# S4 convolution and GEGLU block on one Trainium2 core: a tenth table of y exponentials in the place of an early weight read, with the order of the first 1482 places redone

## The chip, the cores and the metric

The kernel runs on one core of a Trainium2 chip. The metric is the device time of one execution in microseconds (us). Within a core, TensorE (PE) multiplies matrices, VectorE (DVE), ScalarE (ACT) and GpSimd (POOL) work on tiles, and DMAs are issued from the queues of SyncE (SP), ACT and POOL. Each engine works through its own instructions in the order in which the program lists them and waits on semaphores for the others.

## The reference

A block with adaptive layer norm: an S4 convolution, then a gated feed-forward layer. L = 2048 tokens, D = 448 channels, N = 256 states per channel, 1792 hidden features. All inputs are float32.

```python
mod = (silu(c) @ w_mod)              # six rows of 448: sa, ca, ga, sb, cb, gb
h = layernorm(x) * (1 + ca) + sa
P = exp(dt * A * l)                  # A = A_re + i A_im, for every channel, state and step l
K = einsum("dn,dnl,dn->dl", C, P, dt * B).real
y = irfft(rfft(h, 2 L) * rfft(K, 2 L))[:L] + h * Dskip
x = x + ga * y
h = layernorm(x) * (1 + cb) + sb
g, u = h @ w_gate, h @ w_up
x = x + gb * ((gelu(g) * u) @ w_down)
```

## The kernel before

**Stages.** In the first 40 us the parameters of the first quarter of the channels are prepared. Then, up to about 341 us, the convolution's kernel K is *generated* in 56 steps of eight channels each, while the transforms of the input and of finished parts of K run beside it. A *tail* to about 381 us ends the transforms, applies the inverse, adds the residual and norms the first 512 tokens. From there to the end come the gate, up and down projections, 512 tokens at a time, in float16 pairs of a high and a low part.

**Generation.** The powers exp(dt A l) are split into magnitudes and angles, and each of these into a coarse and a fine part of l. PE multiplies the prepared operand `lt` (read from the scratch tensor `lh_d`) by the constants `ea` and `rd` into `pg`; ACT turns `pg` into the table `my` (y exponentials, L663, 128 x 1024 float32, 4 KB in a partition) for each step, into the smaller `mx` (x exponentials, L645) for pairs of steps, and into sines and cosines `fg` (L689, L693, L700). DVE multiplies `mx` and `fg` to `tx` (L722) and `my` and `fg` to `ty` (L726), and PE multiplies these to `kg` (L749). Then `kg` is copied to `ke` (L483 on DVE, L481 on ACT), turned by L772 and copied to `ako`, the transforms' operand. Exponentials and sines need different function tables on ACT, so a switch between them is an `ACT_TABLE_LOAD`. The `my` tiles form a ring of `NMY` places in the pool `tabl`: up to that many y exponentials can be done ahead of their products, which allows several of them behind one switch.

**The operand.** `prep` works out the operand of a quarter of the channels on DVE and ACT. Two puts (L596) write it to `lh_d`, a read of ones (L515, task `pad`) fills the rows behind it, and the reads at L621 (`lt0` for magnitudes, `lt1` for angles) fetch it turned. `lt0` waits for the first put and for the ones.

**First weights.** The gate and up weights come in tiles `w` of 128 x 4 x 256 float32 (4 KB in a partition). The function `weight` issues the read (L1332; `w.le` on SP for three early ones, `w.la` on ACT's queue for the next three, then `w.ld` on SP), ACT makes the float16 high part `wr` (L1345), and DVE the low part (L1349, L1350). The very first of them, for `cb` and `k` zero, has its own place in the pool `ahead`, which is there from the start, and no dependence; it is read near 55 us. The others share a ring of three places in `ws`, a pool that is opened when the generation's pools are closed (`ev.end`).

**Tail and first tiles.** The norm's result `xn` (L1451, L1452) of each of four blocks of 128 tokens is cast to its high part `hl` (L483 or L481, task `co.h0`), DVE takes the low part (L1460, L1461), PE turns both (L1470) and ACT or DVE copies them to `ht`. The gate and up tiles of the first half (two of the four blocks) start as soon as these two are turned: each is ten and one matmuls for gate and up (L1530, L1524) into a `pq` tile, of which there are two. ACT's gelu of the gate (L1537, `ge`) and DVE's product with the up part (L1544, `fq`) give the `pq` tile free. Small filler matmuls (L1036, tasks `spin`) run on PE in the tail.

**What sets the order.** Nothing is scheduled at run time. The table `PLACE` gives every task a number, and a letter for its engine where it could run on several (a ACT, d DVE, p POOL, s SP); tasks are written out by ascending number. The list of a name counts its tasks in the order in which the program adds them.

## Time and profile before

| what | value |
|---|---|
| timed runs | 776.79, 777.25, 779.4 us; median 777.25 us |
| profiled execution | 776.06 us, with a span of 774.3 us |
| granted PE clock, mean | 0.995 |
| busy in the span | PE 724.2 us (94%), DVE 591.3 (76%), ACT 459.7 (59%), POOL 8.5 (1%) |
| DMA | 139.87 MB, mean 181 GB/s |

The span runs from the first to the last instruction of the profile; the execution's own time has 1.76 us around it. The share of busy time is a mean over stages that differ: PE is at work for 94% of the span, though in the generation another engine sets the pace. In the prediction, rows of groups give the line, engine, operation, tiles and shape, the count, then busy time and mean nanoseconds of one, then the idle time ahead of the group and what ended it; rows of a timeline give the start, the duration, the engine and line, and in brackets the wait ahead.

### The profile page before, as it was taken

To read this page: it belongs to the slowest core of one execution; us is meant where nothing else is said; L and a number is where in the kernel's file an instruction comes from. 1 tells how busy PE (TensorE), PEld (TensorE's weight loads), DVE (VectorE), ACT (ScalarE), POOL (GpSimd) and SP (SyncE) were. 2 spreads that over 40 slices of the span, in tenths; PEclk is the share of its full clock that TensorE was granted. 3 is DMA by queue.
4 is the path that set the end of the run, shared out by engine and by line. 5 is a ranking of instruction groups with operands and counts; after the bars stand their busy time and mean duration, and the time that the engine had idled before them with its cause. 6 is when DMAs were issued, how large, how long until landed. Compare 5 with 4: busy or idle time off the path is not lost.

```text
span 774.3 us, 19010 instructions
## 1 busy us (share of the span) xinstructions
PE 724.2 (94%) x8166; PEld 442.5 (57%) x8166; DVE 591.3 (76%) x891; ACT 459.7 (59%) x613; POOL 8.5 (1%) x23
## 2 busy tenths in 40 slices
PE   2877889998899999989999999999999999999997
PEld 1333554443677777677874445444694446944487
DVE  6999999999999999979958932578774577144743
ACT  5899999999999999952646620244312433022330
POOL 0000000000000000003000000000000000000000
PEclk9999999999999999999999999999999999999999
DMA  9764777997888687897787791455247224013201
GB/s 265 193 187 160 214 184 222 276 272 236 247 230 252 180 233 239 275 310 208 235 269 257 221 235 79 146 166 211 98 82 211 96 96 136 14 50 99 77 2 60
DMA packets 103950, 139.87 MB, mean 181 GB/s; under 512 B 34388, under 2 KB 85492, under 8 KB 103866
## 3 DMA queue, kind: packets, MB, share of 16 engines
q1 hardware_dynamic: 100436, 132.53, 58.2%
q10 hardware_dynamic: 2950, 5.38, 2.0%
q8 instruction: 64, 1.05, 0.6%
q0 software_dynamic: 480, 0.75, 0.3%
q14 instruction: 20, 0.16, 0.1%
HBM read 100.39 MB, written 36.01 MB: 176 GB/s over the span
## 4 chain that ended last, share of the span: by engine, by line
PE 73%; ACT 12%; DVE 8%; DMA 4%; issue 2%; SPq 1%; DVEq 0%; ACTq 0%
PE pq L1530 32%; PE pq L1630 9%; PE pd L1599 4%; PE pg L676 4%; PE pf L1104 4%; PE kg L749 3%; ACT my L663 3%; DVE ty L726 2%; PE pq L1524 2%; PE pf L985 2%; PE pf L1093 2%; PE kg L772 2%; PE pf L1206 2%; ACT fg L689 2%; DMA us<-uo 2%
## 5 line engine op out<-in xcount | busy, mean ns | idle before, releaser
L1530 PE MATMUL pq<-ht,wr 128*128 128x512 f16 (+1 forms) x1200 | 248.3, 365 | 0.1
L1530 PEld LDWEIGHTS <-wr 128*128 128x128 f16 x1200 | 114.6, 98 | 128.5 <-issue 11.3
L726 DVE TENSOR_TENSOR ty<-my,fg 128x2048 f32<-128x2048 f32 x56 | 127.3, 2284 | 0.4 <-ACT fg L693 0.3
L1537 ACT ACTIVATE ge<-pq 128x512 f32<-128x512 f32 (+1 forms) x60 | 34.0, 566 | 106.9 <-PE pq L1524 71.3
L1544 DVE TENSOR_TENSOR fq<-ge,pq 128x512 f32<-128x512 f32 (+1 forms) x60 | 39.0, 650 | 72.6 <-PE pq L1530 45.0
L1556 ACT ACTIVATE hh<-fq 128x1024 f16<-128x1024 f32 (+1 forms) x49 | 46.7, 962 | 65.6 <-DVE fq L1544 47.0
L1630 PE MATMUL pq<-d,hh 128*128 128x224 f16 x476 | 68.9, 259 | 0.0
L722 DVE TENSOR_TENSOR tx<-mx,fg 128x1024 f32<-128x1024 f32 x56 | 67.6, 1218 | 0.2 <-ACT fg L700 0.2
L749 PE MATMUL kg<-ty,tx 128*32 128x64 f32 x3584 | 61.6, 222 | 4.4 <-DVE tx L722 1.7
L749 PEld LDWEIGHTS kg<-ty,tx 128*32 128x32 f32 x3584 | 53.2, 111 | 21.3 <-issue 5.9
L1559 DVE TENSOR_TENSOR hlo<-fq,hh 128x1024 f16<-128x1024 f32 (+1 forms) x49 | 53.7, 1106 | 12.9 <-ACT hh L1556 12.7
L1630 PE MATMUL pq<-d,hlo 128*128 128x224 f16 x238 | 61.6, 259 | 0.0
L689 ACT ACTIVATE fg<-pg 128x1024 f32<-128x1024 f32 x56 | 57.6, 1040 | 0.5 <-PE pg L676 0.3
L663 ACT ACTIVATE my<-pg 128x1024 f32<-128x1024 f32 x56 | 56.2, 1032 | 0.4
L1630 PEld LDWEIGHTS <-hh 128*128 128x128 f16 x560 | 54.1, 98 | 0.9 <-issue 0.2
L693 ACT ACTIVATE fg<-fg,small 128x1024 f32<-128x1024 f32 x36 | 42.2, 1180 | 0.0
L1104 PE MATMUL pf<-q,fc 128*128 128x160 f32 x264 | 41.5, 307 | 0.0
L1104 PEld LDWEIGHTS pf<-q,fc 128*128 128x128 f32 x264 | 36.5, 190 | 5.3 <-issue 2.2
L676 PEld LDWEIGHTS <-lt 64*128 64x128 bf16 x304 | 17.7, 95 | 35.0 <-issue 22.7
L676 PE MATMUL pg<-ea,lt 64*128 64x512 bf16 x152 | 31.3, 390 | 6.5 <-ACT fg L689 3.0
L1747 ACT ACTIVATE d<-fq 128x896 f16<-128x896 f32 x14 | 13.2, 946 | 39.7 <-PE pd L1599 27.3
L985 PE MATMUL pf<-ui,fu 128*128 128x448 f32 x66 | 31.2, 576 | 1.2 <-DVE uo L993 0.5
(210 smaller groups left out, 1119.2 us busy)
## 6 DMA issues: line engine op xcount, KB each, us to landing
wr<-w_d SPq DMA_DIRECT2D x21, 896.0 KB, 4.6
fc<-in_k_fc SPq DMA_DIRECT2D x20, 576.0 KB, 4.2
u_d<-so SPq DMA_DIRECT2D x32, 224.0 KB, 3.0
ui<-u_d SPq DMA_DIRECT2D x10, 672.0 KB, 6.0
fq<-in_wd SPq DMA_DIRECT2D x14, 448.0 KB, 4.1
w<-in_wgu SPq DMA_DIRECT2D x11, 512.0 KB, 4.6
us<-uo SPq DMA_DIRECT2D x22, 240.0 KB, 4.5
q<-us SPq DMA_DIRECT2D x22, 240.0 KB, 4.5
```

What stands on the lines that cost most here:

```text
L663: A.activation(yb.tile.rearrange("p h (n k) -> p n h k", n=2), pb.tile.rearrange("p (n h k) -> p n h k", n=2, h=2), AF.Exp)
L676: T.matmul(pa[:, nh * 512:nh * 512 + 512], w, x, start=(k == 0), stop=(k == 2))
L689: A.activation(fb.tile[:, 0].rearrange("p x (n k) -> p n x k", n=2), pb.tile.rearrange("p (n x k) -> p n x k", n=2, x=2), AF.Sin, scale=TW ...
L722: V.tensor_mul(tx.tile, xb.tile[:, xm, None, :].to_broadcast([128, 2, 512]), fb.tile[:, :, 0])
L726: V.tensor_mul(ty.tile, yb.tile[:, :, None, :].to_broadcast([128, 2, 2, 512]), fb.tile[:, None, :, 1].to_broadcast([128, 2, 2, 512]))
L749: T.matmul(kg[32 * g:32 * g + 32, 2 * (s % 2) + q, :64], tx[:, r, nh, 4 * q + g], ty[:, 0:4:3, nh, 4 * q + g] if r else ty[:, 1:3, nh, 4 * ...
L985: T.matmul(pb.tile, fu.tile[:, i], ui.tile[:, EORD[e0 + i] % 32 - s0], start=True, stop=True)
L1104: T.matmul(pz.tile[:, e % 32 - sl0], fc.tile[:, i, 1 + t], pp.tile[:, t, i], start=(t == 0 and e != 32), stop=(t == 1 and e != 0))
L1530: T.matmul(pb.tile[k][:, ts], wr.tile[:, 4 * lo + t, k, c0:c0 + 128], ht[:, m, ts], start=f % 2 == 0 and i == 0, stop=f % 2 == 1 and i == 9)
L1556: A.activation(hg.tile[0][:, cb, c], fq.tile[:, c], AF.Copy)
L1559: V.tensor_sub(hg.tile[1][:, cb, c], fq.tile[:, c], hg.tile[0][:, cb, c])
L1630: T.matmul(bank(k)[:, m], x[:, p, q[0], ts], w[:, p, q[1]], start=new and m == 0 and p == 0 and z == 0, skip_group_check=True, stop=i in ( ...
```

## The change

The ring `my` gets ten places in `tabl` instead of nine. In `weight`, the case of the very first tile is gone: it takes a place of the ring `ws` like its neighbours, and its read waits for the end of the generation (`EV["end"]`) and for `t_x`, a task of the tail. `PLACE` has new numbers for the tasks up to about place 1481, and some tasks change between ACT and DVE; from 1482 on the order is as before. The code below `weight` moves up by one line, so L1332 becomes L1331, and so on.

```diff
-    NMY, NMX = 9, 5
+    NMY, NMX = 10, 5
...
         early = cb + k < 2 and cb < 2
-        zero = cb + k == 0
 
         def ld():
-            wb.tile = (ahead if zero else POOLS["ws"]).tile([128, 4, 256], FT, name="w")
+            wb.tile = POOLS["ws"].tile([128, 4, 256], FT, name="w")
             (dma if early or cb >= PRE else adma)(wb.tile, a["wgu"][cb, :, k])
...
-            t1 = add("w.le", {"SP": 0.42}, -1350 + k + 2 * cb, ld, [] if zero else [EV["end"], t_x], [wb], kb=540)
+            t1 = add("w.le", {"SP": 0.42}, -1350 + k + 2 * cb, ld, [EV["end"], t_x], [wb], kb=540)
...
-    "w.le": "196 1300 1323",
+    "w.le": "1284 1311 1310",
...
-    "co.h0": "1393d 1404a 1432d 1435a",
+    "co.h0": "1395a 1404a 1437a 1436d",
```

Three places of the order bear on the prediction. The first is SP's queue at the start of the program: the read of ones (L515) and the first put (L596, 112x1536), with the reads of the constants `au`, `rd`, `ea` and of the operand `lt`. Before:

```order
L806 DMA fg<-in_w_mod 112x1792 x3
L515 DMA lh_d<-in_k_one 224x512
L596 DMA lh_d<-lh 112x1536
L487 DMA au<-in_k_au 128x128
L487 DMA rd<-in_k_rd 128x1025
L487 DMA ea<-in_k_ea 128x1536
L621 DMA lt<-lh_d 64x7x128 x2
```

After:

```order
L806 DMA fg<-in_w_mod 112x1792 x3
L596 DMA lh_d<-lh 112x1536
L515 DMA lh_d<-in_k_one 224x512
L487 DMA rd<-in_k_rd 128x1025
L487 DMA ea<-in_k_ea 128x1536
L487 DMA au<-in_k_au 128x128
L621 DMA lt<-lh_d 64x7x128 x2
```

The ones now stand behind the put.

The second is ACT where the gate and up tiles begin: the gelus `ge` of the first tiles, the cast `hl` of a block, its turned copies `ht`, the weight read `w` and the conversion `wr`. Before:

```order
L481 ACTIVATE hl<-xn 128x448
L481 ACTIVATE hl<-xn 128x64
L1537 ACT_TABLE_LOAD
L1537 ACTIVATE ge<-pq_5471 128x256
L481 ACTIVATE ht<-pd 128x4x128
L1537 ACTIVATE ge<-pq_5501 128x256
L481 ACTIVATE ht<-pd 128x4x128
L1537 ACTIVATE ge<-pq_5568 128x256
L481 ACTIVATE ht<-pd 128x4x128
L1345 ACTIVATE wr<-w 128x4x256
```

After:

```order
L1536 ACT_TABLE_LOAD
L1536 ACTIVATE ge<-pq_5472 128x256
L1331 DMA w<-in_wgu 128x1024
L1536 ACTIVATE ge<-pq_5517 128x256
L481 ACTIVATE hl<-xn 128x448
L481 ACTIVATE hl<-xn 128x64
L481 ACTIVATE ht<-pd 128x4x128
L1358 DMA w_d<-wr 128x3584
L481 ACTIVATE ht<-pd 128x4x128
L1344 ACTIVATE wr<-w 128x4x256 x2
L1536 ACTIVATE ge<-pq_5578 128x256
```

The cast moved from ahead of the first gelu to behind the second, the weight read from earlier to between them, and two conversions stand ahead of the third gelu where one stood behind it.

The third is DVE in the same stretch, with the casts and low parts of the normed blocks (`hl`), the products `fq` and the low parts `wr` of the weights. Before:

```order
L483 CAST hl<-xn 128x448
L483 CAST hl<-xn 128x64
L1460 TENSOR_TENSOR hl<-xn,hl 128x448
L1461 COPY hl<-hl 128x64
L1544 TENSOR_TENSOR fq<-ge,pq_5472 128x256
L1349 SCALAR_TENSOR_TENSOR wr<-w,wr 128x3x256
L1350 SCALAR_TENSOR_TENSOR wr<-w,wr 64x256
L1544 TENSOR_TENSOR fq<-ge,pq_5502 128x256
```

After, from the second product to the third:

```order
L1543 TENSOR_TENSOR fq<-ge,pq_5518 128x256
L1459 TENSOR_TENSOR hl<-xn,hl 128x448
L1460 COPY hl<-hl 128x64
L1459 TENSOR_TENSOR hl<-xn,hl 128x448
L1460 COPY hl<-hl 128x64
L1348 SCALAR_TENSOR_TENSOR wr<-w,wr 128x3x256
L1349 SCALAR_TENSOR_TENSOR wr<-w,wr 64x256
L483 COPY ht<-pd 128x4x128
L1348 SCALAR_TENSOR_TENSOR wr<-w,wr 128x3x256
L1349 SCALAR_TENSOR_TENSOR wr<-w,wr 64x256
L1543 TENSOR_TENSOR fq<-ge,pq_5579 128x256
```

Both low parts of the blocks, and two low parts of weights, stand between the second and the third product now.

On PE the order at this point is the same in both: the first tile, the second, the turn of eight blocks of `hl` (L1470 before, L1469 after), then the third.

340 rows, old and new, of the table PLACE are left out of this document.

## The prediction, made before the change was run

> **What bounds the kernel now.** I read the table of windows first, cut where the character of the work changes; its columns are the window, its length, the busy time of PE, PEld, DVE, ACT and POOL with instruction counts, the granted PE clock, the DMA share and GB/s.
>
> ```profile
> 0.00:10.00 10.00, 0.00 (x0) 0.00 (x0) 4.38 (x14) 4.38 (x9) 0.88 (x10) 1.00 0.81 268
> 10.00:40.00 30.00, 20.97 (x80) 8.43 (x81) 27.60 (x62) 24.46 (x34) 0.00 (x0) 0.94 0.78 207
> 40.00:341.00 301.00, 275.36 (x5132) 175.64 (x5133) 294.47 (x338) 290.35 (x362) 0.00 (x0) 0.99 0.80 232
> 341.00:381.00 40.00, 38.48 (x488) 32.48 (x480) 33.49 (x70) 15.97 (x34) 7.58 (x13) 1.00 0.73 213
> 381.00:700.00 319.00, 319.00 (x1988) 179.95 (x1986) 195.42 (x350) 107.07 (x153) 0.00 (x0) 1.00 0.50 153
> 700.00:774.30 74.30, 70.37 (x495) 45.97 (x494) 35.99 (x60) 17.42 (x24) 0.00 (x0) 0.99 0.16 51
> ```
>
> Row three is the generation of the S4 kernel. DVE is busy 294.47 of 301 us and ACT 290.35, so DVE sets the pace, with 6.5 us idle, and ACT follows closely. Row four is the tail: the last transforms, the convolution's output and the norm ahead of the gate and up projections; PE has 1.5 us idle. From 381 us PE has no gap for 319 us. The order of the program is unchanged from shortly after that point, so a delay of the first gate and up matmuls goes to the end in full, and nothing the change does later can help.
>
> The next view, the groups, says where the tables stand in this, and the list of DVE's waits says what the 6.5 us are:
>
> ```profile
> L726 DVE TENSOR_TENSOR ty<-my,fg 128x2048 f32<-128x2048 f32 x56 | 127.3, 2284 | 0.4 <-ACT fg L693 0.3
> L663 ACT ACTIVATE my<-pg 128x1024 f32<-128x1024 f32 x56 | 56.2, 1032 | 0.4
> L722 DVE TENSOR_TENSOR tx<-mx,fg 128x1024 f32<-128x1024 f32 x56 | 67.6, 1218 | 0.2 <-ACT fg L700 0.2
> ```
> ```profile
> DVE q L1097 <- PE pf L1093: 1.5, 3, 0.7
> ...
> DVE tx L722 <- ACT fg L700: 0.2, 1, 0.2
> ```
>
> The last figures of the group rows are idle time ahead of the group: ACT stood 0.4 us in all ahead of its 56 y exponentials, and DVE 0.4 us ahead of the 56 products that use the tables. So nobody waits for a tenth table now. The list of waits has 13 rows from the first to the last shown, together 5.2 us, and none of them names `my`.
>
> **The change, part by part.** *The tenth table.* Counting y exponentials issued less y products issued in the two orders, at most nine tables were held before, and ten are held now, but the tenth only once. The switches between exponentials and sines stay: 43 table loads on ACT in both. The table is therefore worth what a shifted ACT order is worth. DVE's work up to the last `tx` product, counted with the mean duration of each form, goes from 353.29 to 353.53 us (these means overlap a little at the ends); ACT's to its last sine differs by 0.07. So the generation costs +0.2 by work. Its waits can fall by at most the 5.2 us listed and can grow by as much; none of the listed waits is removed by a rule of the change, so I take 0 for them, with both ends kept.
>
> *The start.* The copy of ones into the transposed operand (L515) is issued before the first put (L596) now, and behind it after the change. The first read of `lt` (L621) needs both.
>
> ```profile
> 5.88 0.65 SPq L515 DMA_DIRECT2D lh_d<-in_k_one  x1
> 18.25 0.33 SPq L596 DMA_DIRECT2D lh_d<-lh  x1
> ...
> 22.05 1.34 SPq L621 DMA_DIRECT2D lt<-lh_d  x2
> ```
> ```profile
> DMA to landing us min/median/max: 3.7/6.6/6.8
> ```
> ```profile
> DMA to landing us min/median/max: 7.7/7.7/7.7
> ```
> ```profile
> 25.90 1.28 ACT L663 ACT_TABLE_LOAD   x1
> 27.19 1.02 ACT L663 ACTIVATE my<-pg 128x1024 f32<-128x1024 f32 x1
> ```
> ```profile
> 25.23 0.71 PE L658 MATMUL pg<-ea,lt 64*128 64x512 bf16 x2
> 19.27 0.62 DVE L878 BATCH_NORM_STATS2 st<-xt 128x6 f32<-128x448 f32 x1
> ```
>
> The two landing rows are those of L596 (eight issues) and of L515 (four). The put is the step that `lt` waits for: 18.25 + 3.7 is 21.95, and the read starts at 22.05. After the change DVE has one more pair of statistics (0.62 + 0.18 us) ahead of the product that the put sends, so the put starts near 19.05 and the ones near 19.45. If they land in 3.7 us, `lt` is read at 23.2, 1.1 later. The first exponentials have cover for that: their matmul ends at 25.94, but ACT, held by a table load, starts them at 27.19, 1.25 later. That gives 0. If the ones need the 7.7 us of their only reading (a later copy, in the generation, where puts take 6.6 as well), the read starts at 27.2, 5.2 later, and 3.9 are left behind the cover. I take 0, since the put at 3.7 us is the nearest row in time, queue and target, and keep 3.9 as the upper end. [...]
>
> *The first weights.* Their read goes from near 55 us to the tail, behind the end of the generation, and their table of 4 KB no longer has a place of its own. ACT is busy 15.97 of 40 us in the tail and needs them 30 us later, so the read and its conversion lie in idle time: 0, and if the cover were gone, a landing of some 5 us. SP carries one DMA of 512 KB more in the tail ahead of the early read of the convolution's result: about 0.5 us of issue, an estimate from the 0.33 that such an issue takes on ACT's queue below and the 0.65 of L515 above, on a step whose first matmul is at 361.20, with other PE work on both sides. Also 0.
>
> *The tail.* The generation hands over here, and PE picks up:
>
> ```profile
> 339.54 1.22 DVE L722 TENSOR_TENSOR tx<-mx,fg 128x1024 f32<-128x1024 f32 x1
> 344.50 1.60 PE L1188 MATMUL pf<-ako,fc 128*128 128x128 f32 x12 [0.70 <-ACT ako L481]
> 361.20 0.76 PE L1404 MATMUL pd<-yi,ai 128*64 128x320 f32 x4
> ```
>
> From 344.5 to 380.8 PE runs with hardly a gap and the same matmuls in both orders, some of them filler, until the last normed block is turned. On that chain the cast of the first block moves from DVE (0.49) to ACT (0.72), and two small DVE steps of the last block stand behind a neighbour's. I work out +0.35 us for the first gate matmuls, with ends 0 and 1.5 (PE's idle time there, once more).
>
> *The first gate and up tiles.* Here the new order puts a wait where there was none.
>
> ```profile
> 380.80 2.34 PE L1530 MATMUL pq<-ht,wr 128*128 128x256 f16 x20
> 382.91 0.72 ACT L481 ACTIVATE hl<-xn 128x448 f16<-128x448 f32 x2 [1.00 <-DVE xn L1452]
> 383.40 2.36 PE L1530 MATMUL pq<-ht,wr 128*128 128x256 f16 x20
> 384.29 0.49 DVE L483 CAST hl<-xn 128x448 f16<-128x448 f32 x2
> 384.94 0.38 ACT L1537 ACTIVATE ge<-pq 128x256 f32<-128x256 f32 x1
> 385.60 0.61 PE L1470 MATMUL pd<-idenh,hl 128*128 128x128 f16 x8
> 386.04 2.35 PE L1530 MATMUL pq<-ht,wr 128*128 128x256 f16 x20
> ```
>
> Before, the third block's cast (`hl`, ACT at 382.91) was ready 2 us before PE turned it at 385.60, straight behind the second tile. After, ACT's order is first gelu, weight read, second gelu, then that cast. The second gelu needs the second tile complete, and PE's next instructions are the turn. So PE stands while ACT does 0.38 of gelu and 0.72 of cast, with some 0.1 of hand-over: 1.2 us. No other work is queued on PE between, and the gelu can't start sooner, so I count it in full. It is the largest term and the firmest.
>
> *The third weights.* Their read on ACT's queue (L1332, whose landing is the last row here) stands behind the first gelu after the change, and their conversion ahead of the third:
>
> ```profile
> 379.27 0.33 ACTq L1332 DMA_DIRECT2D w<-in_wgu  x1
> 389.46 1.05 ACT L1345 ACTIVATE wr<-w 128x1024 f16<-128x1024 f32 x1
> 390.55 0.96 DVE L1349 SCALAR_TENSOR_TENSOR wr<-w,wr 128x768 f16<-128x768 f32 x1 [0.74 <-ACT wr L1345]
> 391.52 0.42 DVE L1350 SCALAR_TENSOR_TENSOR wr<-w,wr 64x256 f16<-64x256 f32 x1
> 389.05 0.42 DVE L1544 TENSOR_TENSOR fq<-ge,pq 128x256 f32<-128x256 f32 x1 [0.73 <-ACT ge L1537]
> ```
> ```profile
> DMA to landing us min/median/max: 3.9/4.6/5.3
> ```
>
> Shifted by the terms above, the first gelu ends near 384.2, the read lands near 389.0, two conversions (1.05 each) run on ACT to about 391.15 and the low part (0.96 + 0.42) on DVE to about 392.9. The third product (0.42) stands behind it and ends at 393.3; PE needs its buffer for the fifth tile at about 391.55 + 1.55 = 393.1. That is +0.3 with rounding up, 0 if the read lands at 3.9, and +1 at 5.3 with the gelus of that stretch queued behind.
>
> *Sum.* 0.2 + 0 + 0 + 0.35 + 1.2 + 0.3 = **+2.05 us** on the profiled execution's 776.06 (774.3 of span and 1.76 around it), or 778.1. The median of the three timed runs is 777.25, 1.2 higher, and the prediction is of such a median: **779.3**.
>
> **The rivals.** *Faster: the generation's waits go.* DVE's 5.2 us of listed waits, 1.5 of it for the inverse transform's matmuls at L1093, depend on what stands beside what, and the whole order ahead of the tail is new. If it empties all of them and the tail costs the +2 above, the time is 777.25 + 2.05 − 5.2 = 774.1. It is below no change's bound (2.3 us, see below) from 4.4 us of gain on, and any less lands within it. For it: 10.6 us of ACT's time in that window is idle too, so neither engine is at its limit. Against it: nothing in the change removes the matmuls or the ACT steps that end those waits, and DVE's work is 0.2 longer.
>
> *No change: the stall is made up.* If ACT is ready earlier in the tail and 1 to 2 us of waits go in the generation, the sum is 0 to +1: 777.3 to 778.3.
>
> *Slower: the ones land late.* By their own reading of 7.7 us the exponentials start 3.9 later. DVE can fill only part of that with statistics and copies (27.60 of 30 us busy already); by the rest, 2 to 3.9, the time is 781.3 to 783.2. It decides from a landing of about 4.9 us on.
>
> *The clock.* It falls in one place:
>
> ```profile
> 32.00:34.00 2.00, 1.76 (x10) 0.50 (x9) 1.97 (x5) 1.97 (x6) 0.00 (x0) 0.66 0.99 293
> 34.00:36.00 2.00, 1.80 (x8) 0.71 (x8) 1.97 (x7) 1.98 (x3) 0.00 (x0) 0.50 0.42 152
> ```
>
> That follows windows in which PE was idle some 40%. If the new stall brought the same 0.5 for 4 us, it would cost another 2 us: 781.3. Against it, a gap of 1.2 us among full windows is far shorter than that stretch. [...]
>
> *The table doesn't do what it says.* The tenth is held once, and ACT waited only 0.4 us for anything there; then the table is worth nothing by itself and what is left is the order. My forecast contains this.
>
> **How the numbers follow.** Forecast as summed (778.1 to 780.5): 0.40. Faster by the waits: 0.17, of which 0.12 past the bound. No change, made up: 0.15. Ones late: 0.18. New waits in the generation: 0.06. Clock: 0.04. A measurement of this kernel can tell about 0.3% (2.3 us) from no change, so faster means under 774.9 and slower over 779.6. Of the forecast's case 0.15 lies above the latter. Faster 0.12, same 0.25 + 0.05 + 0.15 = 0.45, slower 0.15 + 0.18 + 0.06 + 0.04 = 0.43. The range from 775.0 to 782.3 leaves out most of the gain past the bound and the upper part of the late ones, less than 0.2 together.
>
> **What would show it.** The turn (L1469 after the change) behind the second gate tile starts about 1.2 us after that tile, waiting for ACT's `hl`: the stall. The last `tx` ends at 340.8 ± 0.5: the generation; far below, and the waits rival holds. The first y exponential starts at 27.2: the start; at 29 to 31, the ones land late. The group of y exponentials still has idle time near 0.4: the table changed nothing by itself. If the turn has no wait, or the end of the generation moves by over 2 us either way, the prediction is wrong.

## The result, and the profile after

The changed kernel takes 789.72 us in the median of four runs (787.27 to 792.91), the kernel before 778.09 us in the median of four beside them. The ratio is 1.0149 with a 95% interval of 1.012 to 1.0179: slower by some 11.6 us, far outside the predicted range. The profiled execution is the fastest of the four, 787.27 us with a span of 785.2 us, 10.9 us more than before's span.

The table of windows of the changed kernel, cut like that of before:

```profile
10.00:40.00 30.00, 20.34 (x74) 8.74 (x75) 25.44 (x57) 22.36 (x33) 0.00 (x0) 0.90 0.79 209
40.00:341.00 301.00, 273.69 (x5099) 174.05 (x5099) 292.41 (x338) 291.05 (x362) 0.00 (x0) 0.99 0.80 227
341.00:381.00 40.00, 34.63 (x454) 29.37 (x443) 28.37 (x48) 11.55 (x23) 6.98 (x12) 0.96 0.71 201
381.00:700.00 319.00, 316.99 (x2013) 181.99 (x2014) 198.01 (x362) 109.34 (x162) 0.69 (x1) 1.00 0.51 155
```

DVE is idle for 4.56 us of the second window (2.40 before) and 8.59 of the third (6.53). The large difference is in the window of the tail: PE is busy 34.63 us there, 38.48 before. So the loss is not mainly where the tables are made.

Six points that every profile here has cut the span into stages. The differences of their starts, before and after:

| stage | before | after | more |
|---|---|---|---|
| start to the first `tx` product (L722) | 41.20 | 42.99 | 1.79 |
| first to last `tx` product | 298.34 | 299.45 | 1.11 |
| last `tx` product to last kernel matmuls (L749) | 1.27 | 5.54 | 4.27 |
| from there to the first transform of the tail (L1188) | 3.69 | 3.69 | 0 |
| from there to the matmuls that end the convolution (L1409, after: L1408) | 27.98 | 31.27 | 3.29 |
| from there to the first gate matmul (L1530, after: L1529) | 8.32 | 8.22 | -0.10 |
| from there to the end of the span | 393.50 | 394.04 | 0.54 |

They add up to the 10.9. **The third stage** in the timeline of PE (start, duration, line, tiles, count, and the wait ahead in brackets), first before:

```profile
336.43 3.50 PE L1104 MATMUL pf<-q,fc 128*128 128x160 f32 x24
340.81 1.10 PE L749 MATMUL kg<-ty,tx 128*32 128x64 f32 x64 [0.88 <-DVE tx L722]
341.84 1.97 PE L772 MATMUL kg<-ak,ke 128*64 128x128 f32 x32
```

Here two groups of the transform run through, and the last kernel matmuls wait for nothing but the last `tx` product. After, with the last `tx` product on DVE at 342.44:

```profile
340.35 1.10 PE L749 MATMUL kg<-ty,tx 128*32 128x64 f32 x64
341.38 0.40 PE L1104 MATMUL pf<-q,fc 128*128 128x160 f32 x1
344.75 3.30 PE L1104 MATMUL pf<-q,fc 128*128 128x160 f32 x11 [2.97 <-issue]
347.98 1.10 PE L749 MATMUL kg<-ty,tx 128*32 128x64 f32 x64
351.67 1.60 PE L1188 MATMUL pf<-ako,fc 128*128 128x128 f32 x12 [0.70 <-ACT ako L481]
```

A group of 12 matmuls of one transform stops behind its first matmul for 2.97 us. "Issue" says that PE waited for nothing that the profile shows, and the program has no wait between the matmuls of one group. The other eleven then take 3.30 us, where a whole group of twelve, at 338.52, took 1.90. The windows of one microsecond say why (the third number from the end is the granted clock):

```profile
343.00:344.00 1.00, 0.00 (x0) 0.00 (x0) 1.00 (x3) 0.00 (x0) 0.00 (x0) 1.00 1.08 377
345.00:346.00 1.00, 1.00 (x5) 1.00 (x6) 0.00 (x0) 0.00 (x0) 0.00 (x0) 0.50 0.98 363
346.00:347.00 1.00, 1.00 (x5) 1.00 (x5) 0.00 (x0) 0.00 (x0) 0.00 (x0) 0.50 0.76 307
```

From 344.50 on, a quarter of a microsecond before the gap ends, the clock is at 0.50 for 3.41 us. The last kernel matmuls wait behind all this, though their operand was ready at 343.66.

**The fifth stage** in the timeline of all engines, after:

```profile
372.03 0.42 SPq L1139 DMA_DIRECT2D fg<-in_k_ft  x1
372.56 0.37 SPq L1223 DMA_DIRECT2D yb_d<-z  x1
374.02 6.74 SPq L1296 DMA_DIRECT2D yi<-yb_d  x6
382.94 0.66 PE L1408 MATMUL pd<-yi,ai 128*64 128x128 f32 x8 [2.83 <-DMA yi<-yb_d]
```

The last rows `z` of the convolution go through DRAM (`yb_d`) into `yi`. Ahead of their last store SP issues a read of transform constants (480 KB), the six reads of `yi` leave SP over 6.74 us, and PE waits 2.83 us for them. Before, PE had no wait there:

```profile
370.63 1.91 PE L1206 MATMUL pf<-my,fg 128*96 128x128 f32 x16
372.48 0.66 PE L1409 MATMUL pd<-yi,ai 128*64 128x128 f32 x8
```

**The start**, in the timelines of SP, PE and ACT:

```profile
19.22 0.32 SPq L596 DMA_DIRECT2D lh_d<-lh  x1
19.58 0.65 SPq L515 DMA_DIRECT2D lh_d<-in_k_one  x1
23.76 1.35 SPq L621 DMA_DIRECT2D lt<-lh_d  x2
26.89 0.87 PE L658 MATMUL pg<-ea,lt 64*128 64x512 bf16 x2 [0.95 <-DMA lt<-lh_d]
27.84 1.02 ACT L663 ACTIVATE my<-pg 128x1024 f32<-128x1024 f32 x1
```

The put is 0.97 us later than before, `lt` is read 4.2 us behind the ones, and the first y exponential starts at 27.84, 0.65 later.

**The stall that was predicted** between the second and the third gate tile isn't there:

```profile
393.76 2.36 PE L1529 MATMUL pq<-ht,wr 128*128 128x256 f16 x20
395.06 0.38 ACT L1536 ACTIVATE ge<-pq 128x256 f32<-128x256 f32 x1 [0.46 <-PE pq L1529]
395.35 0.71 ACT L481 ACTIVATE hl<-xn 128x448 f16<-128x448 f32 x2
395.97 0.62 PE L1469 MATMUL pd<-idenh,hl 128*128 128x128 f16 x8
396.43 2.35 PE L1529 MATMUL pq<-ht,wr 128*128 128x256 f16 x20
```

The second gelu starts at 395.06, in the middle of the tile's 20 matmuls, and PE turns the block as soon as the tile ends.

At last, the other users of the tenth place. The ring `my` doesn't hold y exponentials alone: the operands of the last transforms (L1137, L1149) and their products have the same tag. Their first reads before, then after:

```profile
310.81 1.07 SPq L1149 DMA_DIRECT2D my<-us  x2
330.56 1.67 SPq L1137 DMA_DIRECT2D my<-in_k_ft  x2
```
```profile
295.13 0.33 SPq L1149 DMA_DIRECT2D my<-us  x1
315.46 0.33 SPq L1137 DMA_DIRECT2D my<-in_k_ft  x1
```

In the new order they go out some 15 us earlier, beside the end of the generation: 47.3 and 27.0 us ahead of the last `tx` product, where before it was 28.7 and 9.0. The tenth place by itself doesn't do this. In c_before_order, the experiment below that has ten places in before's order, they go out 28.7 and 9.0 us ahead as well. Whether the new order needs the tenth place for it was not run.

### The profile page after: what moved, and what is told of

The parts are those of the page before. It is cut to its first block, busy times and chain, and to the rows that moved or that the text cites. A ratio compares the mean times of both kernels' runs of the same rounds, so it can differ in the third digit from the quotient of the medians.

```text
span 785.2 us, 19021 instructions
## 1 busy us (share of the span) xinstructions
PE 726.9 (93%) x8166; PEld 444.6 (57%) x8166; DVE 590.8 (75%) x890; ACT 459.7 (59%) x614; POOL 8.5 (1%) x23
## 3 DMA queue, kind: packets, MB, share of 16 engines
q8 instruction: 64, 1.05, 0.6%
## 4 chain that ended last, share of the span: by engine, by line
PE 73%; ACT 11%; DVE 8%; DMA 4%; issue 3%; SPq 1%; ACTq 0%; DVEq 0%
PE pq L1529 31%; PE pq L1629 9%; PE pf L1104 5%; PE pd L1598 4%; PE kg L749 4%; PE pg L676 4%; PE pf L1093 3%; ACT my L663 2%; PE pq L1523 2%; PE kg L772 2%; PE pf L985 2%; ACT fg L689 2%; PE pd L1629 2%; DMA fg<-in_w_mod 2%; DVE ty L726 1%
## 5 line engine op out<-in xcount | busy, mean ns | idle before, releaser
L1529 PE MATMUL pq<-ht,wr 128*128 128x512 f16 (+1 forms) x1200 | 248.4, 365 | 0.0
L1529 PEld LDWEIGHTS <-wr 128*128 128x128 f16 x1200 | 114.5, 98 | 128.4 <-issue 10.8
L722 DVE TENSOR_TENSOR tx<-mx,fg 128x1024 f32<-128x1024 f32 x56 | 67.9, 1220 | 0.5 <-PE kg L749 0.3
L749 PE MATMUL kg<-ty,tx 128*32 128x64 f32 x3584 | 61.4, 220 | 6.0 <-ACT ako L481 2.6
L749 PEld LDWEIGHTS kg<-ty,tx 128*32 128x32 f32 x3584 | 52.7, 110 | 25.0 <-issue 11.0
L1104 PE MATMUL pf<-q,fc 128*128 128x160 f32 x264 | 43.4, 315 | 3.0 <-issue 3.0
```

Of the source, the lines that this page charges most:

```text
L722: V.tensor_mul(tx.tile, xb.tile[:, xm, None, :].to_broadcast([128, 2, 512]), fb.tile[:, :, 0])
L749: T.matmul(kg[32 * g:32 * g + 32, 2 * (s % 2) + q, :64], tx[:, r, nh, 4 * q + g], ty[:, 0:4:3, nh, 4 * q + g] if r else ty[:, 1:3, nh, 4 * ...
L1104: T.matmul(pz.tile[:, e % 32 - sl0], fc.tile[:, i, 1 + t], pp.tile[:, t, i], start=(t == 0 and e != 32), stop=(t == 1 and e != 0))
L1529: T.matmul(pb.tile[k][:, ts], wr.tile[:, 4 * lo + t, k, c0:c0 + 128], ht[:, m, ts], start=f % 2 == 0 and i == 0, stop=f % 2 == 1 and i == 9)
```

## The experiments

My theory was that three or four places lose time separately: the start, the gap ahead of the last kernel matmuls, the wait for `yi`. The rivals: all of it follows from the late start; or the code without the new order costs the time.

All ratios are against runs of the kernel before on the same chip. The other columns are stages of the one profiled execution, in us, as in the table above. Line numbers in these kernels differ by up to 31 from those above, since their table of places is printed in fewer lines.

| kernel | ratio, 95% interval | first `tx` | first to last `tx` | last `tx` to kernel matmuls | L1188 to L1409 |
|---|---|---|---|---|---|
| after_again | 1.0121 (1.0083 to 1.016) | 43.99 | 302.49 | 3.32 | 31.14 |
| c_before_order | 1.002 (0.9998 to 1.0043) | 43.14 | 301.29 | 1.27 | 29.07 |
| h_bstart_arest | 1.0111 (1.007 to 1.0153) | 43.85 | 302.35 | 1.27 | 31.23 |
| h_astart_brest | 1.0015 (0.9987 to 1.0043) | 44.89 | 302.80 | 1.27 | 27.96 |
| h_agen_btail | 1.0079 (1.0037 to 1.0121) | 44.33 | 300.47 | 2.42 | 29.78 |
| h_bgen_atail | 1.0011 (0.9992 to 1.003) | 43.49 | 298.85 | 1.27 | 28.37 |
| m1_fd_early | 1.0102 (1.0063 to 1.0141) | 44.89 | 304.11 | 5.13 | 29.91 |
| m4_fd_at_fc | 1.0089 (1.0058 to 1.0121) | 44.96 | 298.68 | 1.27 | 28.37 |
| m4_pad | 1.0064 (1.0044 to 1.0084) | 43.54 | 299.46 | 1.27 | 28.37 |
| m4_pad_inv | 1.0083 (1.0052 to 1.0114) | 45.00 | 303.25 | 1.27 | 28.27 |
| m2_reads_late | 1.0102 (1.0063 to 1.0141) | 43.97 | 299.38 | 1.27 | 32.13 |
| m12_both | 1.0151 (1.0117 to 1.0186) | 44.77 | 299.30 | 2.79 | 33.66 |
| m12_pad | 1.0169 (1.0128 to 1.0209) | 43.66 | 302.68 | 1.67 | 33.67 |
| p_pad_late | 1.0002 (0.9984 to 1.002) | 43.93 | 299.08 | 1.27 | 27.97 |
| s_shift88 | 1.0117 (1.0089 to 1.0145) | 43.67 | 300.51 | 4.59 | 29.93 |
| s_shift32 | 1.0189 (1.0163 to 1.0215) | 44.70 | 300.07 | 1.27 | 31.28 |
| b_shift32 | 1.0058 (1.0036 to 1.0081) | 42.22 | 304.93 | 1.27 | 27.97 |
| b_shift88 | 1.0007 (0.9985 to 1.0028) | 40.86 | 300.03 | 1.28 | 27.97 |

In s_shift88 the fifth column goes to the 35 kernel matmuls behind a gap; the first 29 start at 1.27. A profile can be far from the median of its kernel: those of m4_fd_at_fc (780.9, median 786.3) and s_shift32 (786.7, median 793.6) are the fastest of five, that of m1_fd_early (795.5, median 787.7) the slowest.

**The change again, and the change without its order.** The second leaves all tasks in before's order but the first weights' read and conversion.

```diff
 NMY, NMX = 10, 5
-w.le 0 at 196
 ev.end (1249)
+w.le 0
 yi.e (1273)
+w.hi 0
 w.hi 2 (1363)
```

> The changed kernel once more, unaltered, for a second profile of it beside other kernels on one chip. All theories: 1.010 to 1.017 of before. Theory (PE runs out of instructions at fixed points of its stream): the gap with nothing to wait for comes again with 11 matmuls of the last L1104 group left, its length anywhere from 0 to 3 us; the wait of L1408 for yi of some 2.8 us comes again.

> The change without its order: the order of before, with ten tables and with the first weights read (ahead of the early read of yi) and converted in the tail. Theory (the loss is the new order's alone): within 0.3% of before, and no wait on PE for w, nor a longer stretch from the last tx product to the first gate matmul than before's 41.3 us. Rival (the late weights delay the tail, as their 512 KB stand ahead of yi on SP): 1 to 3 us slower.

The second profile of the changed kernel has the gap again with 11 matmuls left, 2.67 us long, and the wait for `yi`, 2.7 us:

```profile
348.10 1.76 PE L1104 MATMUL pf<-q,fc 128*128 128x160 f32 x11 [2.67 <-issue]
384.63 1.12 PE L1408 MATMUL pd<-yi,ai 128*64 128x128 f32 x8 [2.70 <-DMA yi<-yb_d]
```

The clock is the other way round here: the 11 matmuls run at full speed (1.76 us, not 3.30), so the third stage costs 2.0 us more than before and not 4.3. The matmuls behind the wait for `yi` run at half the clock (1.12 us for eight, where the first profile had 0.66), and the stage to the first gate matmul takes 9.62 us, where the first profile had 8.22. The code without the order is at 1.002 with an interval that just takes in 1: most of the loss is the order's. The rival of late weights isn't ruled out, for 0.2% are 1.6 us and it stood for 1 to 3: the tail's stage is 1.1 longer in this profile, with PE waiting 1.1 us for a transfer. Room and late weights together are what is measured here, and the place moves no read in this order.

**Which part of the order.** Heads and rests of the two orders were joined:

```diff
+h_bstart_arest: before's places 0 to 221, then all that is left, in after's order
+h_astart_brest: after's places 0 to 219, then all that is left, in before's order
+h_agen_btail:   after's places 0 to 1249, then all that is left, in before's order
+h_bgen_atail:   before's places 0 to 1250, then all that is left, in after's order
```

> The first 222 places (some 80 us) in the order of before, all that is left in the order of after, ten tables, first weights read behind the generation. Theory (three separate losses: start of the generation +2.9 us, PE without instructions at the generation's end +4.3, wait for the convolution's result in the tail +2.8 and some 0.9 besides): the start's 2.9 go, the others stay, so 2 to 4 us below after's 787 to 790, near 785. Rival (all of it follows from the late start, the rest being its echo): near before's 778.

> The first 220 places in the order of after, all that is left in the order of before, nine tables, first weights read early as in before. Theory: only the start's loss is left, DVE's last tx product 2 to 4 us later than before's 339.5 us, near 781. Rival (all follows from the start): near after's 787 to 790. Second rival (the start costs nothing by itself): 778.

> After's order up to the generation's end (its first 1250 places), then before's order, ten tables, first weights read and converted in the tail. Theory: start and generation's end cost as in after (+7 at the first transform matmul behind the generation), the wait of some 2.8 us for the convolution's result goes: 784 to 787. Rival (the tail is only late because the generation is): same as after, 787 to 790.

> Before's order up to the generation's end (its first 1251 places without the first weights), then after's order, ring of ten, first weights read in the tail. Theory: only the tail's loss is left, +3, with a wait for the convolution's result (yi from yb_d) ahead of the matmuls that end the convolution: near 781. Rival (the tail's order costs nothing where the generation is on time): 778.

After's start by itself is at 1.0015 with an interval across 1, and before's start doesn't save the rest (1.0111): the rival that all follows from the late start falls. After's tail behind before's generation costs nothing that can be measured (1.0011), against my theory's 3 us: its tail takes 28.37 us, not 31.3. So the tail's loss needs after's order up to the generation's end as well. The order suggests why: the 480 KB read (task `t.fd`, number 4) stands at place 1332 in after, and at 1243, ahead of the cut, in before. In h_agen_btail the wait is gone (0.20 us left), but its stage is still 29.78 us; smaller waits of PE stand there, up to 0.73 us each, and were not followed.

The tail has one more cost, which the two profiles of the changed kernel don't show. In six of the thirteen profiles with after's tail, PE waits 0.6 to 2.2 us in all behind the first gate matmul, for a later part of `yi` or for `ht`; in the seven with before's tail it never does. From the first gate matmul to the end it is 395.7 us in h_bgen_atail and 395.5 in m4_pad, where before it was 393.5. In m4_pad most of that is one wait:

```profile
412.18 0.44 PE L1378 MATMUL pd<-yi,ai 128*64 128x128 f32 x4 [1.33 <-DMA yi<-y]
```

**The read ahead of the last z.** It was moved twice.

```diff
 t.fc 4 (1264)
+t.fd 4        m4_fd_at_fc
 f.st 21 (1265)
...
 w.le 1 (1311)
+t.fd 4        m1_fd_early
...
 yi.l1 0 (1331)
-t.fd 4 (1332)
 t.i0 8 (1333)
```

> After, with one 480 KB read of the transform's constants (t.fd number 4, L1139) issued right behind the early weight reads instead of just ahead of the last z's store and the reads of yi on the same queue. Theory (this read delays the z's on their way through DRAM): the 2.8 us wait of L1408 for yi goes, the stretch from the first L1188 to the first L1408 falls from 31.3 to about 28.4 us, time 2 to 3 below after's, near 786 on a chip where after takes 789. Rival (the z's are late by PE and DVE order): stretch stays 31.

> After, with the same 480 KB read (t.fd number 4) issued right behind its first half (t.fc 4), at the end of the generation; in m1_fd_early it still went out only 0.3 us ahead of the last z's, as it waited on SP. Theory (this read delays the last z's way through DRAM): wait for yi under 1 us, the stretch from the first L1188 to the first L1408 28.0 to 28.8 us, as in before, not 31.3; time 2 to 3 below after_again. Rival (z and yi are late by the new order of PE, ACT and the queues): stretch over 30.

In m1 the read had to wait on SP (7.1 us, which the list of SP's waits puts down to a store of `z`) and left 0.4 us ahead of the last z's again: 1.47 us of the wait were left. In m4 the stage takes 28.37 us, the same as with before's generation, and PE has no wait:

```profile
375.14 1.91 PE L1176 MATMUL pf<-my,fg 128*96 128x128 f32 x16
376.98 0.66 PE L1378 MATMUL pd<-yi,ai 128*64 128x128 f32 x8
```

The convolution's last matmuls follow without idle time. The two kernels built on m4, m4_pad and m4_pad_inv, have no wait there either, and every other profile that joins after's generation end to after's tail has one of 1.47 us or more. So the 2.8 us come from this read's place. The time fell from 1.0121 to 1.0089, as much as expected, though the intervals overlap.

**The reads ahead of the gap.**

```diff
-t.u 3 (1256), t.fd 7 (1259), t.fc 3 (1263), t.fc 4 (1264)
 f.st 21 (1265)
+t.u 3, t.fd 7, t.fc 3, t.fc 4
```

> After, with four reads (t.u number 3, t.fd 7, t.fc 3 and 4) issued behind the last store of the transforms, that is behind the end of the generation, instead of in the 8 us before it. Theory (PE's instruction refill queues behind these reads): PE's gap with nothing to wait for at L1104 shrinks from 1.0 to 3.0 us to under 0.7, and the last kgen ends 1.3 us behind the last tx product begins, not 2.4 to 5.5; 1 to 4 us below after's time, if the tail doesn't wait for the late reads. Rival (the refill takes this long whatever the DMAs do): gap stays 1.0 to 3.0.

> After with both edits. Theory: both gains add, 4 to 7 us below after's, near 782 to 784; left over before's time are the start (about 1) and 1 to 3 us. Rival (one loss hides the other): no better than the better of the two.

> As before with both edits, and the read of ones (L515) back ahead of the first put. Theory: the first y exponential starts 0.7 to 1.0 us earlier than in the kernel with both edits (as it does in the orders with before's start), time lower by as much. Rival (the start is set by ACT's order, not by the ones): no change in the start.

In m2 the gap went and the last kernel matmuls started 1.27 us behind the last product; in m12_both, with the same reads late, it was 2.14 us long. One profile each way doesn't show that these reads make the gap. What the change would have brought was lost again in the tail (32.13 to 33.67 us), where PE waited 3.69 to 5.23 us ahead of the matmuls that end the convolution; how the late reads bring that about isn't shown. So m12_both came out at 790 us and not near 782 to 784, and m12_pad started its first y exponential 1.28 us earlier than m12_both (27.80 for 29.08) without being faster.

**The position in PE's stream.** The gap lies at the same matmul in every profile of after's order that has it (one matmul later in h_bstart_arest, where the start is before's). That speaks for the supply of PE's instructions, which is my inference, as no view says whom a packet of instructions is for. The pages of before and after list a queue q8 of the kind "instruction" with 64 packets, 1.05 MB, so 16 KB each; PE has 16332 matmuls and weight loads in both, 255 for each packet if they are PE's. In after's profile, gaps with the cause "issue" at 210.29, 331.16 and 344.75 us lie 2291 and 254 matmuls apart, with 18 and 2 packets from one to the next: 127 for each packet. In after_again such gaps lie 509, 509, 255 and 254 matmuls apart, 4, 4, 2 and 2 times 127 to 128. To move the points and nothing else, idle matmuls were put at the start of PE's stream, where PE has no data yet:

```diff
+dum = keep.tile([128, 64], BF, name="dum")
+P.memset(dum, 0.0)
+dps = gen.tile([128, 1024], FT, name="pg")
+for _ in range(88):                      # 32 in the kernels named shift32
+    T.matmul(dps[:64, :64], dum, dum, start=True, stop=True)
 t_ld = sp("c.ld", -9, ...)
```

> After, with 88 idle 64x64 matmuls (and their weight loads, 176 instructions) at the start of PE's stream, where PE waits for its first data anyway. Theory (refills of PE's instructions at fixed points, 256 instructions apart): the points move by 40 matmuls to later ones, so the last gap is no more in the L1104 group but in the last kgen behind it, which waits for the last tx product first and so hides it; last kgen ends 1.3 to 2 us behind the start of the last tx, and the time is 1 to 4 us below after_again. Rival (something at that place of the program makes PE wait): gap again with 11 matmuls of L1104 left.

> After, with 32 idle matmuls (64 instructions) at the start of PE's stream. Theory (refill points are fixed in the stream): the point moves 32 matmuls towards the front, from 11 left of the last L1104 group into the kgen ahead of it, with 32 or 33 of its 64 left; the last transform and the last kgen have some 1.6 us of slack behind it, so of a gap of up to 3 us at most 1.4 reach the last kgen. Rival: the gap stays at 11 left of L1104.

The timeline of PE in s_shift88, at the end of the generation:

```profile
342.21 1.87 PE L1079 MATMUL pf<-q,fc 128*128 128x160 f32 x12
345.45 0.64 PE L724 MATMUL kg<-ty,tx 128*32 128x64 f32 x29 [1.38 <-DVE tx L697]
348.77 1.28 PE L724 MATMUL kg<-ty,tx 128*32 128x64 f32 x35 [2.67 <-issue]
```

The gap has left the transform and lies in the last kernel matmuls behind it, with 35 of 64 left: 11 + 29 = 40 matmuls later, to the matmul what was forecast (128 less 88). So in these profiles the gap's place goes with the count of PE's instructions, and I call such places refill points. The packets' times agree: in all 23 gaps of over 0.9 us with this cause, from 40 to 400 us in the twenty profiles, PE went on 2.2 to 2.8 us after the start of an instruction packet, 1.2 to 1.6 us after its end (2.74 and 1.41 at 328.30 in before, 2.76 and 1.57 at 331.16 and 2.18 and 1.21 at 344.75 in after). That PE waited for the packet fits these times; no view shows it. But the gap was not hidden by the wait for `tx`, as I had expected: it lasted 2.67 us all the same, and the time was 1.0117. With 32, the point at 3 left of an earlier transform came to 29 left of the kernel matmuls ahead of it, again as many as were added; no gap was seen at the last point. Its time was the longest of all, 1.0189, where at most 1.4 us of a gap had been expected to matter: other refill points may have come to bad places. Its profile shows one, a gap of 1.78 us at 123 us, and the next pair shows a longer one there.

> Before, with 32 idle 64x64 matmuls (64 instructions) at the start of PE's stream. Theory (refill points are fixed in the stream): the gap of 1.0 to 1.5 us with 9 matmuls of a turn (L772) left moves 32 matmuls to the front, into the kgen ahead of it with some 21 of 64 left. If positions are worth time in this order as they seemed in s_shift32 (+0.7% against after), the time differs from before's by over 0.3%, either way. Rival (the slow s_shift32 had another cause): within 0.3%.

> The same with 88 idle matmuls: points 40 matmuls later, that gap behind the turn and one more transform into the kgen that follows, some 45 of 64 left. Theory and rival as for b_shift32; if one of the two is faster than before, the refill points are a means to gain time with no change to the work.

With 64 idle instructions and no other edit, the kernel *before* is slower by 0.58% (0.36 to 0.81); with 176 no change can be measured. The gap with 9 matmuls of a turn left came, 1.50 us long, with 25 left of the kernel matmuls ahead (32 earlier; I had counted the place as 21). A worse one is new. The timeline of PE and ACT in b_shift32:

```profile
120.93 0.38 PE L681 MATMUL pg<-ea,rd 64*128 64x512 bf16 x2
124.14 0.61 PE L681 MATMUL pg<-rd,lt 64*128 64x512 bf16 x2 [2.83 <-issue]
124.79 1.02 ACT L694 ACTIVATE fg<-pg 128x1024 f32<-128x1024 f32 x1 [1.22 <-PE pg L681]
```

It hits the matmuls of the angles, for which ACT waits. The windows of the same kernel around it:

```profile
120.00:121.00 1.00, 1.00 (x60) 0.79 (x49) 0.97 (x2) 0.97 (x3) 0.00 (x0) 1.00 1.05 376
123.00:124.00 1.00, 0.00 (x0) 0.00 (x0) 0.00 (x0) 0.57 (x1) 0.00 (x0) 0.75 0.00 0
124.00:126.00 2.00, 1.86 (x4) 0.94 (x4) 0.00 (x0) 1.21 (x2) 0.00 (x0) 0.50 0.03 8
```

The DMA share was 1.04 to 1.11 from 118 to 121, an instruction packet came at 121.5, 11.7 us behind the last one, and PE went on 2.6 us after it, with the clock at 0.50. Neither version is faster than before.

**The start, and the rest of after's loss.**

```diff
 p.put0 0
+pad 0          p_pad_late, in before's order; there pad 0 stood ahead of it
...
+pad 0          m12_pad, m4_pad and m4_pad_inv, in after's order
 p.put0 0 (38)
-pad 0 (39)
...
-f.inv 21 (1229), f.z 21 (1239)      m4_pad_inv
 kgen 55, ka 26, ka 27, kout 27 (1231 to 1245)
+f.inv 21 behind ka 27, f.z 21 behind kout 27
```

> Before, with the one edit that the read of ones (L515) of the first quarter stands behind the first put. Theory (lt waits for the ones): the first matmul waits for lt and the first y exponential starts 0.3 to 1.9 us later than in before's orders on the same chips (27.8 to 28.5), the time is 0 to 2 us longer. Rival (the cover of 1.25 us holds, as predicted): no wait for lt, no change.

> m4_fd_at_fc with the ones ahead of the first put again. Theory: wait for lt gone, wait for yi gone; left are the instruction gap (0 to 4 us) and the later start of the products (1 us): 1.005 to 1.009 of before. Rival (the losses come back elsewhere): 1.010 or more.

> m4_pad, with the last inverse transform (L1104, f.inv 21) behind the last kgen's turn instead of ahead of the last kgen. The refill point then falls on the 2nd matmul of the last kgen, which waits for the last tx product anyway. Theory (the refill is asked for independently of that wait, and so passes beside it): last kgen ends 1.3 to 2.5 us behind the start of the last tx, and the time is below m4_pad's by what the gap was there. Rival (a refill only begins when PE reaches the point): gap of 1 to 3 us inside the last kgen, nothing won, and the transform comes later by 2 us.

In before's order the ones may stand behind the put: no wait for `lt` above 0.2 us, and no change (1.0002). In after's, where the put itself is a microsecond later, PE waits 0.95 us for `lt` in the first profile and 1.9 in the second, and with the ones in front 0.3 at most; m4_pad is at 1.0064, m4 at 1.0089, with intervals that overlap. In m4_pad the last kernel matmuls come without a gap:

```profile
341.48 2.18 PE L1074 MATMUL pf<-q,fc 128*128 128x160 f32 x12
344.27 1.10 PE L719 MATMUL kg<-ty,tx 128*32 128x64 f32 x64 [0.61 <-DVE tx L692]
```

But the ones alone don't set the start: m4_pad_inv has them in front as well, and its put left at 21.1 and its first y exponential started at 30.05. Taking the transform from ahead of the last kernel matmuls (m4_pad_inv) keeps the gap away too in its one profile, but the transform then stands ahead of the tail:

```profile
349.52 1.10 PE L719 MATMUL kg<-ty,tx 128*32 128x64 f32 x64 [2.42 <-DVE tx L692]
350.55 3.27 PE L742 MATMUL kg<-ak,ke 128*64 128x128 f32 x32
353.76 2.21 PE L1074 MATMUL pf<-q,fc 128*128 128x160 f32 x12
```

The turn of the kernel takes 3.27 us here where it took 1.97, as the clock is at 0.50 behind the wait of 2.42, and the tail starts 6.29 us behind the last kernel matmuls, not 3.69. Nothing was won (1.0083).

No kernel here beats the one before.

## Why the prediction was wrong, step by step

**The tail was the step that failed.** The prediction said that from 344.5 to 380.8 PE runs "with hardly a gap and the same matmuls in both orders", and took +0.35 us with ends of 0 and 1.5. For the hand-over ahead of it, from 339.54 to 344.5, whose rows it shows, the sum had no term. From the last `tx` product to the first gate matmul it was 41.26 us before and 48.72 after: +7.46. Equal work and no gaps before don't say that there are none after. Two new waits made the difference: the gap with the cause "issue" ahead of the last kernel matmuls (4.27 us with the clock at 0.50 behind it), and the wait for `yi` behind a 480 KB read (2.83). The second could have been read from SP's order, where that read stood between the last stores of `z` and the reads of `yi`. The first could not be read from the order, though the trace of before held the sign of it, a gap of 1.49 us inside the turn L772 with "issue" as its cause, ending at 328.3 us, where PE had time to spare. Two signs that the prediction named as showing it wrong both came: the turn has no wait, and the last `tx` starts 2.90 us later.

**The tenth table.** "Nobody waits for a tenth table", and that it is held only once, was right for y exponentials and wrong for the ring. I counted one of its users; the reads of the last transforms use it too, and in the new order they go out beside the generation's end. In before's order the room moves none of them, and with the late weights it costs 0.2%, or at most 0.43 by the interval (c_before_order). The rival that the table is worth nothing and only the order counts was the nearest to what happened.

**The stall of 1.2 us**, "the largest term and the firmest", was 0. The step that failed was that the second gelu needs the second tile complete. It needs the gate half, the first ten of the 20 matmuls, which is done half-way; gelu and cast end with the tile. The terms behind it were right in size in the two profiles of the change: from the first gate matmul to the end it is +0.5 and +0.2, where +0.3 with ends 0 and 1 stood for the third weights. The waits of up to 2.2 us in the kernels with the same tail had no term.

**The start** was taken as 0 with an upper end of 3.9. The mechanism was right in before's order, where the ones behind the put cost nothing (1.0002). In after's own order the put was later, at 19.22, as forecast (19.05), but `lt` was read 4.2 us behind the ones, not 3.7, and DVE was idle for 2.2 us more between 10 and 40 us. The 4.2 are of the first profile; in the nine others with after's start and the ones behind the put they are 3.5 to 3.9, as forecast, while the put left at 18.9 to 21.0. So the late put is the larger part of the delay of `lt`, and what makes it later than 19.05 in most of them stays open. The first `tx` came 1.79 later, or about 1.4 by the means of the eight profiles with after's start and the ones behind the put (44.35, the shifted kernels left out) and the four with before's (42.92).

**The generation** was +1.1 in the first profiles for a forecast of +0.2 by work, and the orders' profiles overlap (298.3 to 302.8 us for before's, 298.7 to 304.1 for after's). A term of this size can't be told from that scatter, for or against the forecast.

**The first weights** cost nothing on their own that can be told from the 0.2%.

**The clock.** That it falls in one place before was a misreading. The trace of before has it at 0.50 again from 60 to 63 us, where PE had no wait over 0.7 us in the five microseconds ahead:

```profile
61.00:62.00 1.00, 1.00 (x38) 0.83 (x32) 1.00 (x5) 1.00 (x2) 0.00 (x0) 0.50 1.02 344
```

What stays open: why the gap is 0 to 3 us long at the same point of the same order. In the ten profiles with after's order at the generation's end (the shifted kernels left out), the last kernel matmuls start between 1.27 and 5.54 us behind the last product, 2.6 in the mean, and in the five with before's order 1.27 each time. The DMA engines were about 0.8 to 1.0 busy in the eight microseconds ahead of it in both. About half of the loss is undone by two moves (1.0121 for the change, 1.0064 for m4_pad); of the other half, the parts of the gaps, of the start and of the waits behind the first gate matmul were not measured by themselves.

## What to carry to other kernels

A pool's extra place can go to whoever shares its tag: list all users of the ring, with their reads, before saying what the place is worth. Where PE works without gaps, read the queue of each producer in the new order (a large read ahead of small stores and of the reads that wait for them), and see on which half of a tile a consumer waits. Gaps with the cause "issue" belong on the list as well: here 32 idle matmuls ahead of before's work cost 0.58%, and 88 cost nothing that can be measured. So an honest test of a small edit has a second version of it with some idle instructions more.

## What the runs showed of the hardware that was not expected

PE stood still with nothing to wait for, at places that go with the count of its instructions: the gap came 40 matmuls later with 88 added ahead (s_shift88), and 32 earlier with 32 (s_shift32's earlier point, and b_shift32 in before's order). That fits refills every 127 to 128 matmuls with their weight loads, which is an inference from these counts. In the gaps of over 0.9 us PE went on 2.2 to 2.8 us after an instruction packet's start, and in b_shift32 the packet came 11.7 us behind the one before, with a DMA share of 0.89 to 1.11 from 112 to 121. The gap of 2.83 us there put the `tx` products from 0.87 us behind before's to 6.41: the clock there was at 0.50 from 124 to 130 us. That is one profile; the time of the kernel is 0.58% longer, or 4.5 us.

In these profiles the granted clock doesn't follow from the length of the gap alone. It was at 0.50 behind after's gap of 2.97 us, but shorter gaps had the same behind them, 1.94 us in after and 1.45 in c_before_order. The end of each gap, and a window behind it:

```profile
71.14 0.39 PE L658 MATMUL pg<-ea,lt 64*128 64x512 bf16 x2 [1.94 <-ACT my L663]
72.00:73.00 1.00, 1.00 (x12) 1.00 (x10) 0.97 (x3) 0.92 (x2) 0.00 (x0) 0.50 0.00 0
```
```profile
203.60 1.17 PE L1063 MATMUL pf<-ako,fc 128*128 128x160 f32 x6 [1.45 <-DMA fc<-in_k_fc]
205.00:206.00 1.00, 1.00 (x8) 0.34 (x6) 1.00 (x2) 0.00 (x0) 0.00 (x0) 0.50 1.13 303
```

Longer ones did not always: after's wait for `yi` of 2.83 us and the gap of 2.67 in the second profile (after_again) had it at 1.00 behind them, while b_shift32's gap of 2.83 brought 0.50. Three waits were longer, 3.69 us in m2_reads_late, 5.22 in m12_pad and 5.23 in m12_both, and all have the clock at 0.50 at their end or just behind. What decides it for the shorter ones stays open. Of the stretches at 0.50 that start between 40 and 700 us, the one in before (at 59.93) and the two in after (at 71.44 and 344.50) took 3.41 us each, and the one behind b_shift32's gap 6.83, from 123.5 on.
